# Fetching the first rows with TensorE instead of a DMA, and running the first two blocks on the whole array

## The chip, the cores and the metric

The kernel runs on one core of a Trainium2 chip. The metric is the device time of one execution, in microseconds. Before the change it is 734.75 us, the median of three runs (734.42 to 734.97). The profile comes from a further execution of 734.93 us, in which the core's instructions span 733.2 us; TensorE's granted clock was at full speed throughout.

## The reference

A dynamic convolution over tokens feeds a feed-forward layer with a squared ReLU. `B, S, D = 8, 4096, 192`, with `H = 8` heads of 24 features and `K = 7` taps; the hidden layer has 2048 features.

```python
w = softmax(weight_gen, axis=-1)                    # (B, S, 8, 7)
x_pad = concatenate([zeros(B, 6, D), x], axis=1)
# every token is a weighted sum of itself and the 6 tokens before it;
# the 24 features of one head share the weights
out[b, s, h, :] = sum_k w[b, s, h, k] * x_pad[b, s + k, h, :]
h = maximum(out @ w_in, 0)                          # (32768, 192) @ (192, 2048)
result = h * h @ w_out                              # (32768, 2048) @ (2048, 192)
```

## The kernel before

The tokens go through in blocks: blocks 0 and 1 have 512 tokens each, all others 1024. For each block the kernel does this:

- softmax of the taps on ScalarE and VectorE, into rows `v` (64 numbers for a token: 8 heads with 8 places each);
- "band": the rows of 128 consecutive tokens (`wr`) times a mask give a band matrix `bd` on VectorE, five overlapping tiles for 512 tokens;
- "conv": x times band on TensorE gives `yp`, the convolved tokens with features on the partitions; it is copied out of PSUM into `y`;
- "unit" (`u`): two chunks of 128 hidden features. TensorE computes `h` from `w_in` and `y`, ScalarE takes the ReLU into `t`, VectorE squares it into `g`;
- "M": half of the hidden features of 256 tokens. TensorE multiplies `g` with `w_out` into `o`.

The 192 features do not fill the 128 rows of the array evenly, so the kernel uses three steps of 64 features, and two matmuls stand side by side on the two halves of the rows. For that, `w_in` has to exist a second time with its row halves exchanged (`w_i[:, q, 1]`).

The start, before the first `h`. The softmax has one partition for every 8 tokens (`FIRST = 8`), while the band needs one partition for each token; DMAs do that rearrangement.

```python
# [cut] tiles, helpers
def cross_w_in(q):                      # exchanged halves by DMA
    for r0, r1 in ((0, RT), (RT, 0)):
        nc.sync.dma_start(out=w_i[r0 : r0 + RT, q, 1], in_=w_i[r1 : r1 + RT, q, 0])

def cross_w_in_by_pe(q):                # exchanged halves by a permutation on TensorE
    # [cut] loop over 3 x 512 columns
            nc.tensor.matmul(out=pt[...], lhsT=swap, rhs=w_i[:, q, 0, c : c + TB], ...)
        nc.scalar.copy(out=w_i[:, q, 1, a:b], in_=pt[:, 0 : b - a])

# [cut]
spin(25)                                # TensorE warming matmuls, result unused
half_swap(); band_mask()                # GpSimd
nc.gpsimd.memset(v_big, 0.0)
s0.load(nc.sync)
load_w_in(w_st[0], 0, nc.sync)          # f32, first half of w_in's columns
x_load_f32(0)
load_w_in(w_st[1], 1, nc.sync)
s0.exp(0, s0.rh); s0.total(0, s0.rh); s0.recip(0, s0.rh)
s0.scale(0, s0.rh, nc.vector)           # the rows v are ready here
nc.scalar.copy(out=w_i[:, 0, 0], in_=w_st[0])
wr_load_sbuf(0, [s0], (0, 2, 1, 4, 3), (nc.sync, nc.gpsimd))   # rows of block 0
wr_load_sbuf(1, [s0], range(NT), (nc.gpsimd,))                 # rows of block 1
x_cast(0, nc.scalar.copy)
cross_w_in_by_pe(0)
spin(14)
x_load_f32(1)
nc.scalar.copy(out=w_i[:, 1, 0], in_=w_st[1])
cross_w_in(1)
s1.load(nc.sync)
for i in (0, 2, 1, 3, 4):
    st_band(0, (i,))
st_conv(0)
```

The blocks then follow fixed plans. `B` is a band, `X` a cast of x, `E` and `S` the two halves of a softmax, `C` the convolution of the next block, `L` a load of weights:

```python
plans = {
    0: "B1 X1 u u u E1 S1 u C u u u u",
    1: "L3 u u B2 M E2 B3 u M E2 u u S2 u M u C u S2 M",
    # [cut] the later blocks
}
```

A unit, and the copy of `yp` in block 0:

```python
def st_unit(j, u):
    th = BLOCKS[j][1] * TB // 2         # 256 in blocks 0 and 1, 512 later
    per = TB // th                      # 2 in blocks 0 and 1, 1 later
    # [cut]
    for jj in range(per):
        for slot in range(NK):          # 3 steps of 64 features
            for half, r0 in enumerate((0, RT)):
                k = slot ^ half if slot < 2 else slot
                nc.tensor.matmul(
                    out=h[:, half, jj * th : (jj + 1) * th],
                    lhsT=w_in_chunk(w, u * per + jj, slot, half),
                    rhs=y_t[j][r0 : r0 + RT, k, 0:th], ...,
                    tile_position=(r0, 0),
                )
    # [cut] ReLU and square

# in st_conv, for block 0:
copies = ((0, 2, nc.scalar.copy), (2, NK, nc.vector.tensor_copy))
```

In blocks 0 and 1, `o` uses the full array with 128 rows; from block 2 on it stands on the two row halves.

Of the kernel before, what the change touches and what calls it, by code (L numbers as in the profile page):

```python
# [9 lines left out]
def kernel(  # L10
# [26 lines left out]
    nc = tc.nc  # L37
# [14 lines left out]
    P = 128  # L52
# [2 lines left out]
    NSUB = B * NBB  # L55
    BLOCKS = [(0, 1), (1, 1)] + [(n, 2) for n in range(2, NSUB, 2)]
    NBLK = len(BLOCKS)
    NF = Dff // P

    R = S // P  # L60
# [7 lines left out]
    BASE = -24  # L68
    starts = [BASE + STEP * i for i in range(NT)]
    bounds = [0, 104, 208, 312, 416, TB]  # L70

    AluOp = mybir.AluOpType
    AxisX = mybir.AxisListType.X
# [21 lines left out]
    w_p = const.tile([P, WQ, 2, NQ + NQ // 2], f16, name="w_p")  # L95
    w_o = const.tile([P, NF, Dm], f16, name="w_o")
    mask = const.tile([P, P, 2], f16, name="mask")
    swap = const.tile([P, P], f16, name="swap")
    FIRST = 8
    PARTS = {0: (8, 8, 8, 8), 1: (8, 8, 16), 2: (16, 16)}  # L100
    v_big = const.tile([P, R + 2 * HALO, HP, SL, 2], f16, name="v_big")
    v_first = [
        const.tile([P, FIRST + 2 * HALO, HP, SL, 2], f16, name=f"v_first{i}") for i in (0, 1)
    ]

    def half_swap():

        nc.gpsimd.memset(swap, 0.0)
        for base in (RT, -RT):
            nc.gpsimd.affine_select(  # L110
                out=swap, in_=swap, pattern=[[-1, P]], compare_op=AluOp.not_equal,
                fill=1.0, base=base, channel_multiplier=1,
            )

    def band_mask():

# [22 lines left out]
    def cross_w_in(q):  # L139
        for r0, r1 in ((0, RT), (RT, 0)):  # L140
            nc.sync.dma_start(out=w_i[r0 : r0 + RT, q, 1], in_=w_i[r1 : r1 + RT, q, 0])

    def cross_w_in_by_pe(q):
        n = NQ + NQ // 2
        for a in range(0, n, 2 * TB):
            b = min(a + 2 * TB, n)
            pt = ps_h.tile([P, 2 * TB], f32, name="pt", tag="h")
            for c in range(a, b, TB):
                nc.tensor.matmul(
                    out=pt[:, c - a : c - a + TB], lhsT=swap, rhs=w_i[:, q, 0, c : c + TB],  # L150
                    start=True, stop=True,
                )
            nc.scalar.copy(out=w_i[:, q, 1, a:b], in_=pt[:, 0 : b - a])

    def load_w_spread():

# [197 lines left out]
    def wr_load_sbuf(j, parts, order, engines):  # L354
# [3 lines left out]
        for i in order:  # L358
            t0 = max(j % NBB * TB + tile_start(j, i), 0)
            for s in parts:  # L360
                a, b = max(t0, s.t0), min(t0 + P, s.t0 + P * s.r)
                if a < b:
# [5 lines left out]
                    )  # L368
                    n += 1

    def st_band(j, tiles):


        if j not in bd_t:
            bd_t[j] = p_bd.tile([P, H * NT * STEP], f16, name="bd")
        i = tiles[0]
        lo = STEP * i
        shift = 0 if i == 0 and j % NBB == 0 else lo - tile_start(j, i)
        n = min(STEP, P - shift)
        shape = (P, HP * len(tiles), n // SL, 2 * SL)  # L380
        nc.vector.tensor_tensor(  # L381
            out=bd_t[j][:, H * lo : H * (lo + len(tiles) * n)].rearrange(
                "p (g m c) -> p g m c", g=shape[1], c=2 * SL
            ),
            in0=wr_t[j][:, i : tiles[-1] + 1]
            .rearrange("p t g c -> p (t g) c")
            .unsqueeze(2)
            .broadcast_to(shape),
            in1=mask[:, shift : shift + n]
            .rearrange("p (m c) e -> p m (c e)", c=SL)  # L390
            .unsqueeze(1)
            .broadcast_to(shape),
            op=AluOp.mult,
        )
# [7 lines left out]
    def conv_pieces(j):  # L402


        s0, n = BLOCKS[j]
        th = n * TB // 2
        halves = []
        for half in (0, 1):
            s, a = (s0 + half, 0) if n == 2 else (s0, th * half)
            halves.append([  # L410
                (s, i, half, max(bounds[i], a), min(bounds[i + 1], a + th), a)
                for i in range(NT) if bounds[i] < a + th and bounds[i + 1] > a
            ])
        if n == 2:
            for k in range(NK):
                for later in (True, False):
                    for pair in zip(*halves):
                        for s, i, half, a, b, base in pair:
                            for q in (2 * k, 2 * k + 1):
                                yield later, s, i, q, half, a, b, base  # L420
        else:
            for pair in zip(*halves):
                for later in (True, False):
                    for k in range(NK):
                        for s, i, half, a, b, base in pair:
                            for q in (2 * k, 2 * k + 1):
                                yield later, s, i, q, half, a, b, base

    def st_conv_spread(j):

# [35 lines left out]
    def st_conv(j):  # L466

        if j >= FIRST_SPREAD:
            return st_conv_spread(j)
        n = BLOCKS[j][1]  # L470
        th = n * TB // 2
        per = 1024 // th
        y = p_y.tile([P, NK, TB], f16, name="y")
        y_t[j] = y
        yps = [
            ps_h.tile([P, 2 * TB], f32, name="yp", tag="h") for _ in range(-(-NK // per))
        ]
        for later, s, i, q, half, a, b, base in conv_pieces(j):
            lo = bounds[i]
            hi = lo + (STEP if tile_start(s, i) == starts[i] else bounds[i + 1] - lo)  # L480
            _, ha, hb, pre = quads[q]
            m, h = (32, hb) if later else (pre, ha)
            bd = bd_t[s][:, H * lo : H * hi].rearrange("p (g c e) -> p g e c", g=HP, e=2)
            p0 = RT * half + 32 * (q % 2)
            k = q // 2
            col = th * (k % per) - base
            nc.tensor.matmul(  # L487
                out=yps[k // per][p0 : p0 + m, col + a : col + b],
                lhsT=x_t[s][:, i, 32 * q : 32 * q + m],
                rhs=bd[:, h // 2, h % 2, a - lo : b - lo],  # L490
                start=True,
                stop=True,
                skip_group_check=True,
                tile_position=(0, p0),
            )
        for n, yp in enumerate(yps):
            k0, k1 = n * per, min((n + 1) * per, NK)

            copies = ((k0, k1, nc.scalar.copy),)
            if j == 0:  # L500
                copies = ((0, 2, nc.scalar.copy), (2, NK, nc.vector.tensor_copy))
            for a, b, copy in copies:
                copy(  # L503
                    out=y[:, a:b, 0:th],
                    in_=yp[:, (a - k0) * th : (b - k0) * th].rearrange("p (k c) -> p k c", c=th),
                )

    def st_unit(j, u):

        th = BLOCKS[j][1] * TB // 2  # L510
        per = TB // th
        w = w_p if j >= FIRST_SPREAD else w_i
        h = ps_h.tile([P, 2, TB], f32, name="h", tag="h")
        for jj in range(per):
            for slot in range(NK):
                for half, r0 in enumerate((0, RT)):
                    k = slot ^ half if slot < 2 else slot
                    nc.tensor.matmul(  # L518
                        out=h[:, half, jj * th : (jj + 1) * th],
                        lhsT=w_in_chunk(w, u * per + jj, slot, half),  # L520
                        rhs=y_t[j][r0 : r0 + RT, k, 0:th],
                        start=(jj == 0 and slot == 0), stop=(slot == NK - 1),
                        skip_group_check=True,
                        tile_position=(r0, 0),
                    )
# [22 lines left out]
    def st_mm2(j, qt, fcs, ccs, o):  # L548


        th = BLOCKS[j][1] * TB // 2
        per = TB // th
        half, off = divmod(qt * QT, th)
        for fc in fcs:
            g = g_t[(j, fc // per)][:, half, fc % per * th + off :]
            for cc in ccs:
                n = P // len(o)
                for i, oo in enumerate(o):
# [36 lines left out]
    with nc.allow_low_precision("fp16 matmul pipeline"), tc.manual_schedule():  # L595
# [18 lines left out]
        warm = const.tile([P, TB], f16, name="warm")  # L614
        gate = const.tile([P, 1], f32, name="gate")
        nc.vector.memset(warm, 0.0)
        for v in v_first:
            nc.vector.memset(v, 0.0)

# [2 lines left out]
        def spin(n):  # L622
# [2 lines left out]

        s0, s1, s2 = parts[:3]
        spin(25)
        half_swap()
        band_mask()
        nc.gpsimd.memset(v_big, 0.0)  # L630
        s0.load(nc.sync)
# [1 line left out]
            p_wg.tile([P, (R + HALO) * HK], f32, name="w_st", tag="wg")[:, 0 : NQ + NQ // 2]  # L633
            for q in (0, 1)
        ]
        load_w_in(w_st[0], 0, nc.sync)
        x_load_f32(0)
        load_w_in(w_st[1], 1, nc.sync)
        s0.exp(0, s0.rh)
        s0.total(0, s0.rh)  # L640
        s0.recip(0, s0.rh)
        s0.scale(0, s0.rh, nc.vector)
        nc.scalar.copy(out=w_i[:, 0, 0], in_=w_st[0])
        wr_load_sbuf(0, [s0], (0, 2, 1, 4, 3), (nc.sync, nc.gpsimd))
        wr_load_sbuf(1, [s0], range(NT), (nc.gpsimd,))
        x_cast(0, nc.scalar.copy)
        cross_w_in_by_pe(0)
        spin(14)
        x_load_f32(1)
        nc.scalar.copy(out=w_i[:, 1, 0], in_=w_st[1])  # L650
        cross_w_in(1)
        s1.load(nc.sync)
        for i in (0, 2, 1, 3, 4):
            st_band(0, (i,))
        st_conv(0)

# [1 line left out]
        for q in range(4):  # L658
# [7 lines left out]
        steady = "MuMuuu" * 3 + "MuuuMCu"  # L666
        steady_spread = "MuMuuu" * 2 + "MuCMuuu" + "MuMuuu"
        plans = {
            0: "B1 X1 u u u E1 S1 u C u u u u",
            1: "L3 u u B2 M E2 B3 u M E2 u u S2 u M u C u S2 M",  # L670
            2: "L4 u u u E3 M u u u M B4 u u u u M B5 S3 u u u u M u E3 C u",
            3: "L5 L6 M S3 u u u M u u u u M u M B6 E4 u u u M M B7 u u u E4 M u M C S4 u",
# [109 lines left out]
        for j in range(NBLK):  # L782
            if j + 2 < NBLK:
                load_rows(j + 2)
            u = 0
            for step in plans[j].split():
                kind, n = step[0], int(step[1:] or 0)
# [21 lines left out]
                    st_bands(n)  # L809
                elif kind == "L":  # L810
                    parts[n].load(nc.sync)
                elif kind == "X":
                    x_cast(n, nc.vector.tensor_copy)

# [46 lines left out]
```

The softmax here doesn't subtract the row's maximum and nothing guards it: scores larger than these inputs give would overflow.

## Time and profile before

| What | Value |
|---|---|
| Time, median of three | 734.75 us (734.42 to 734.97) |
| Span in the profile | 733.2 us |
| ScalarE busy in the span | 613.8 us (84%) |
| Warming matmuls, first group | 25, from 1.27 us on |
| Cast of the first half of w_in on ScalarE | 8.06 us, 1.47 us long |
| Start of the first band product | 12.27 us |
| Start of the first `h` matmul | 16.03 us |
| Start of the first square `g` | 19.19 us |
| Start of the first `o` matmul | 26.00 us |
| Start of block 2's first unit | 37.56 us |

How it is read: the page gives busy time by engine for the whole span (PE is TensorE's matmuls, PEld its weight loads, DVE VectorE, ACT ScalarE, POOL GpSimd, SP the engine that issues most DMAs). An engine may be busy without setting the time. So the chain that ended last is read beside it: from the last instruction back to whatever released each step. The share that an engine has in this chain says who sets the end. What happens only in the first 37 us is lost in the averages of a 733 us span; for this the chain, the waits and the busy times are asked of a window, and instructions in order of time. `L381` and the like are lines of the kernel; `x5` is the number of instructions in a group.

### The profile page before, as it was taken

The numbers are of one execution on the slowest core, as the hardware profiler recorded it, in microseconds if no ns is written. First come the engines' busy times: TensorE is split into PE (matmuls) and PEld (weight loads), VectorE is DVE, ScalarE is ACT, GpSimd is POOL, SyncE is SP. The second block draws the span as 40 slices with busy tenths as digits, with TensorE's granted clock in tenths as the row PEclk, the third lists the DMA queues.
The fourth block names the chain that finished last, engine by engine and source line by source line (L and its number), as shares of the span: only waits on it lengthen the run. The fifth ranks groups of instructions, "written<-read, shape, count | busy, mean of one in ns | idle before, by whom it ended". The sixth has DMA issues, their size and how long they took to land.

```text
span 733.2 us, 31124 instructions
## 1 busy us (share of the span) xinstructions
PE 726.3 (99%) x14106; PEld 528.5 (72%) x14106; DVE 627.3 (86%) x856; ACT 613.8 (84%) x724; POOL 100.5 (14%) x148
## 2 busy tenths in 40 slices
PE   8999999999999999999999999999999999999998
PEld 4767777777777777777777777777777777777777
DVE  5999898998898988888988888988889988778753
ACT  5998888988888888888888888888888888888883
POOL 7322222320001100011000010010100110001000
PEclk9999999999999999999999999999999999999999
DMA  7745444794445442455433464334544315444012
GB/s 216 124 88 132 81 63 106 143 164 119 93 73 117 105 86 64 71 131 112 69 70 72 115 125 82 62 68 122 104 87 85 59 49 120 66 87 78 30 45 67
DMA packets 126544, 68.71 MB, mean 94 GB/s; under 512 B 85193, under 2 KB 122636, under 8 KB 125900
## 3 DMA queue, kind: packets, MB, share of 16 engines
q1 hardware_dynamic: 80908, 48.12, 23.0%
q0 software_dynamic: 45360, 18.50, 21.6%
q8 instruction: 110, 1.80, 1.0%
q14 instruction: 22, 0.18, 0.1%
q10 hardware_dynamic: 144, 0.10, 0.0%
HBM read 50.18 MB, written 28.70 MB: 108 GB/s over the span
## 4 chain that ended last, share of the span: by engine, by line
PE 96%; DVE 1%; DMA 1%; ACT 1%; issue 0%; DVEq 0%
PE o L560 47%; PE h L518 45%; PE yp L450 4%; PE yp L487 1%; DVE bd L381 1%; DMA wr<-v_first 1%; ACT t L532 0%; DMA wg<-in_weight_gen_dram 0%; ACT ex L250 0%; DVE v_first L272 0%; ACT y L503 0%; DVE ssum L257 0%; DVE rcp L264 0%; DVE g L536 0%; DVE xt L347 0%
## 5 line engine op out<-in xcount | busy, mean ns | idle before, releaser
L532 ACT ACTIVATE t<-h 128x1024 f16<-128x1024 f32 x512 | 496.5, 1026 | 59.9 <-PE h L518 59.5
L560 PEld LDWEIGHTS <-g 64*128 64x128 f16 (+1 forms) x8032 | 342.5, 94 | 55.9 <-issue 2.5
L560 PE MATMUL o<-w_o,g 64*128 64x192 f16 (+1 forms) x8032 | 379.0, 243 | 0.0
L536 DVE TENSOR_TENSOR g<-t 128x2048 f16<-128x2048 f16 (+1 forms) x309 | 309.3, 1037 | 28.1 <-ACT t L532 27.9
L518 PE MATMUL h<-y,w_p 64*128 64x512 f16 x2400 | 291.7, 376 | 0.0
L518 PEld LDWEIGHTS <-w_p 64*128 64x128 f16 x2400 | 113.8, 94 | 94.9
L381 DVE TENSOR_TENSOR bd<-wr,mask 128x4160 f16<-128x4160 f16 (+3 forms) x89 | 149.4, 1703 | 4.1 <-DMA wr<-v_first 4.1
L576 DVE TENSOR_TENSOR o_sb<-o,o_sb 128x384 f32<-128x384 f32 x123 | 68.4, 556 | 60.8 <-ACT o_sb L574 59.8
L333 POOL DMA_DIRECT2D xt<-in_x_dram x62 | 52.1, 843 | 421.6 <-PE yp L450 362.5
L574 ACT COPY o_sb<-o 128x384 f32<-128x384 f32 x129 | 61.6, 478 | 46.7 <-PE o L560 45.9
L518 PE MATMUL h<-y,w_i 64*128 64x512 f16 (+1 forms) x768 | 82.1, 350 | 1.8 <-ACT t L532 0.8
L518 PEld LDWEIGHTS <-w_i 64*128 64x128 f16 x768 | 36.1, 94 | 28.6 <-issue 4.0
L450 PEld LDWEIGHTS <-xt 128*32 128x32 f16 x2000 | 24.5, 95 | 10.6 <-issue 10.6
L272 DVE TENSOR_TENSOR v_big<-ex,rcp 128x112 f16<-128x112 f32 (+5 forms) x180 | 29.8, 236 | 1.8 <-DMA vd<-v_big 0.8
L460 DVE CAST y<-yp 128x1024 f16<-128x1024 f32 x25 | 30.4, 1218 | 0.0
L450 PE MATMUL yp<-bd,xt 128*32 128x104 f16 (+1 forms) x2000 | 28.3, 210 | 0.0
L250 ACT ACTIVATE ex<-wg 128x560 f32<-128x560 f32 (+4 forms) x38 | 25.9, 682 | 1.7 <-DMA wg<-in_weight_gen_dram 1.7
L257 DVE TENSOR_REDUCE ssum<-ex 128x80 f32<-128x560 f32 (+4 forms) x38 | 25.3, 666 | 2.2 <-ACT ex L250 2.2
L460 ACT CAST y<-yp 128x1024 f16<-128x1024 f32 x25 | 25.2, 1006 | 0.0
L264 DVE RECIPROCAL rcp<-ssum 128x80 f32<-128x80 f32 (+4 forms) x38 | 22.8, 600 | 1.3
L323 POOL DMA_DIRECT2D xt<-in_x_dram x7 | 3.9, 553 | 124.7 <-PE yp L450 109.7
L363 POOL DMA_DIRECT2D wr<-v_first x31 | 16.9, 563 | 16.0 <-DVE v_first L272 15.8
(34 smaller groups left out, 97.3 us busy)
## 6 DMA issues: line engine op xcount, KB each, us to landing
out_dram<-o_sb SPq DMA_DIRECT2D x63, 384.0 KB
xt<-in_x_dram POOLq DMA_DIRECT2D x42, 240.0 KB, 5.0
wg<-in_weight_gen_dram SPq DMA_DIRECT2D x4, 1064.0 KB
xt<-in_x_dram POOLq DMA_DIRECT2D x20, 192.0 KB, 4.7
wr<-vd SPq DMA_DIRECT2D x38, 80.0 KB
vd<-v_big SPq DMA_DIRECT2D x5, 512.0 KB
y<-y SPq DMA_DIRECT2D x100, 24.0 KB
wg<-in_weight_gen_dram SPq DMA_DIRECT2D x5, 392.0 KB
```

What stands on the lines that cost most here:

```text
L250: nc.scalar.activation(out=self.ex[:, lo:hi].rearrange("p r g k e -> p (r g) k e"), in_=self.wg[:, lo:hi].rearrange("p r (g e) k -> p (r g ...
L272: eng.tensor_tensor(out=bass.AP(tensor=v.tensor, offset=v.offset + lo * H * SL + lo % SL * 2 + g * SL * 2, ap=[list(v.ap[0]), [H * SL + 2, ...
L333: eng.dma_start(out=dst[:, first:last], in_=ap)
L381: nc.vector.tensor_tensor(out=bd_t[j][:, H * lo : H * (lo + len(tiles) * n)].rearrange("p (g m c) -> p g m c", g=shape[1], c=2 * SL), in0= ...
L450: nc.tensor.matmul(out=yp[p0 : p0 + 32, k - k0, a:b], lhsT=x_t[s][:, i, c0 : c0 + 32], rhs=bd[:, head // 2, e, 0 : b - a], start=True, sto ...
L460: copy(out=y[:, k0 : k0 + 2], in_=yp)
L518: nc.tensor.matmul(out=h[:, half, jj * th : (jj + 1) * th], lhsT=w_in_chunk(w, u * per + jj, slot, half), rhs=y_t[j][r0 : r0 + RT, k, 0:th ...
L532: nc.scalar.activation(out=t1[:, e], in_=h, func=ActF.Relu)
L536: nc.vector.tensor_tensor(out=g[:, a : e + 1], in0=t1[:, a : e + 1], in1=t1[:, a : e + 1], op=AluOp.mult)
L560: nc.tensor.matmul(out=oo[:, cc * Dm : (cc + 1) * Dm], lhsT=g[r0 : r0 + n, cc * P : (cc + 1) * P], rhs=w_o[r0 : r0 + n, fc, :], start=(fc ...
L574: nc.scalar.copy(out=o_sb, in_=o[0][:, c])
L576: nc.vector.tensor_tensor(out=o_sb, in0=o[1][:, c], in1=o_sb, op=AluOp.add)
```

## The change

It has two parts, both in the first two blocks.

First, the rows of block 0 no longer travel by DMA. A 0/1 matrix `sel` picks from the softmax tile, for each of the five band tiles, the row of each token: 8 accumulating matmuls for a tile (one for each token place in a partition), 64 columns each, into a PSUM tile of its own. ScalarE copies each to `wr`. This is meant to take the DMA's latency out of the start. The rows of block 1 still go by DMA, from two queues now.

Second, blocks 0 and 1 arrange `y` differently. 128 of the features stand on all partitions, so a matmul for them uses the whole array and all 512 tokens; the other 64 features stand twice, once on each row half, and two half-row matmuls run side by side. A unit has 4 matmuls of 512 tokens in place of 12 of 256. No exchanged copy of `w_in` is needed in these blocks, so the permutation on TensorE is dropped and the exchange of both halves by DMA moves to the start of block 1, for use in block 2.

Moves that go with it: x is loaded ahead of `w_in`; x is cast before `w_in`; the second half of `w_in` is cast on VectorE in block 0 (new step `W`); the second group of 14 warming matmuls is gone; the softmax weights of the second part are loaded earlier.

```diff
-    def cross_w_in_by_pe(q): ...                      # [cut]
+    def select_rows(j, s, tiles):
+        wr_t[j] = p_wr.tile([P, NT, HP, SL * 2], f16, name="wr")
+        for n, i in enumerate(tiles):
+            if 0 < n < 4:
+                pr = ps_h.tile([P, H * SL], f32, name="pr", tag="h")
+            else:
+                pr = ps_o.tile([P, H * SL], f32, name="pr", tag=("o1", "o0")[n // 4])
+            a = max(j % NBB * TB + tile_start(j, i), 0) - s.t0
+            for r in range(s.r):
+                c = a + FIRST - 1 - r
+                nc.tensor.matmul(
+                    out=pr, lhsT=sel[:, c : c + P],
+                    rhs=s.v[:, HALO + r].rearrange("p g c e -> p (g c e)"),
+                    start=(r == 0), stop=(r == s.r - 1),
+                )
+            nc.scalar.copy(out=wr_t[j][:, i].rearrange("p g c -> p (g c)"), in_=pr)

+    def st_conv_first(j):                             # [cut] places of the 192 features
+        yp = ps_h.tile([P, 2, TB], f32, name="yp", tag="h")
+        ...
+        if j == 0:
+            nc.scalar.copy(out=y[:, 0], in_=yp[:, 0])
+            nc.vector.tensor_copy(out=y[:, 1], in_=yp[:, 1])
+        else:
+            nc.scalar.copy(out=y[:, 0:2], in_=yp)

+    def first_unit(u, h, y):
+        q, f = divmod(u, NF // WQ // 2)
+        both = [
+            (h[:, n], w_i[:, q, 0, (f + n * NF // WQ // 2) * P :][:, 0:P], y[:, 0], 0)
+            for n in (0, 1)
+        ]
+        upper = [
+            (h[:, n], w_i[r0 : r0 + RT, q, 0, NQ + f * P :][:, 0:P], y[r0 : r0 + RT, 1], r0)
+            for n, r0 in enumerate((0, RT))
+        ]
+        pairs = (upper, both) if u % 2 else (both, upper)
+        ...                                           # [cut] the 4 matmuls

     spin(25)
-    half_swap()
+    row_select()
     band_mask()
     nc.gpsimd.memset(v_big, 0.0)
     s0.load(nc.sync)
+    x_load_f32(0)
     load_w_in(w_st[0], 0, nc.sync)
-    x_load_f32(0)
     load_w_in(w_st[1], 1, nc.sync)
     ...                                               # [cut] softmax, unchanged
+    x_cast(0, nc.scalar.copy)
+    x_load_f32(1)
+    wr_load_sbuf(1, [s0], range(NT), (nc.gpsimd, nc.sync))
+    s1.load(nc.sync)
+    select_rows(0, s0, ROW_ORDER)
     nc.scalar.copy(out=w_i[:, 0, 0], in_=w_st[0])
-    wr_load_sbuf(0, [s0], (0, 2, 1, 4, 3), (nc.sync, nc.gpsimd))
-    wr_load_sbuf(1, [s0], range(NT), (nc.gpsimd,))
-    x_cast(0, nc.scalar.copy)
-    cross_w_in_by_pe(0)
-    spin(14)
-    x_load_f32(1)
-    nc.scalar.copy(out=w_i[:, 1, 0], in_=w_st[1])
-    cross_w_in(1)
-    s1.load(nc.sync)
-    for i in (0, 2, 1, 3, 4):
+    for i in ROW_ORDER:                               # (0, 1, 2, 3, 4)
         st_band(0, (i,))
     st_conv(0)

-            0: "B1 X1 u u u E1 S1 u C u u u u",
+            0: "B1 X1 W u u u E1 S1 u C u u u u",

+            if j == 1:
+                for q in range(WQ):
+                    cross_w_in(q)
+                elif kind == "W":
+                    nc.vector.tensor_copy(out=w_i[:, 1, 0], in_=w_st[1])
```

## The prediction

> **What bounds the kernel now.** I read the page's busy shares first, then the chain that ended last, then the busy time by windows, and only then the start of the span, instruction by instruction, because the change touches nothing after the second block.
>
> ```profile
> PE 726.3 (99%) x14106; PEld 528.5 (72%) x14106; DVE 627.3 (86%) x856; ACT 613.8 (84%) x724; POOL 100.5 (14%) x148
> PE 96%; DVE 1%; DMA 1%; ACT 1%; issue 0%; DVEq 0%
> ```
>
> Over the span TensorE sets the time: 96% of the chain. So a microsecond saved at the start comes out at the end only if TensorE starts its unbroken run earlier, and no other engine holds it up again before that run settles. The windows show where it settles (columns: length, busy PE, PEld, DVE, ACT, POOL with instruction counts, clock, DMA share, GB/s):
>
> ```profile
> 0.00:16.03 16.03, 13.69 (x114) 5.86 (x115) 7.35 (x19) 8.04 (x8) 11.64 (x21) 1.00 0.79 218
> 16.03:26.00 9.97, 8.59 (x192) 6.97 (x192) 9.90 (x20) 8.86 (x11) 5.01 (x8) 1.00 1.18 193
> 26.00:37.56 11.56, 11.56 (x258) 9.65 (x257) 11.47 (x19) 10.44 (x14) 4.54 (x8) 1.00 0.43 73
> ```
>
> The useful TensorE work begins at 16.03 us; block 2 begins at 37.56. What surprised me is VectorE: 9.90 of 9.97 us busy, then 11.47 of 11.56. In blocks 0 and 1 VectorE is as full as TensorE, so whatever the change adds to it there counts. The chain in order of time, for the first 34 us (start, length, what):
>
> ```profile
> 6.70 1.47 DVE v_first L272 x8
> 8.19 3.98 DMA wr<-v_first
> 12.27 2.61 DVE bd L381 x5
> 14.92 0.45 PE yp L487 x16
> 15.40 0.59 ACT y L503
> ...
> 16.36 2.35 DVE bd L381 x2
> 18.70 0.57 DVE xt L347
> ...
> 25.24 0.83 PE h L518 x12
> 26.07 1.43 PE o L560 x16
> ```
>
> The softmax rows are ready at 8.17, the DMA that hands them over takes 3.98 us, the five band products 2.61, the convolution's tail 0.45, the eviction 0.59; then h starts. After that the chain stays on VectorE (bands of the second block, the cast of x), passes through ScalarE and reaches TensorE for good at 25.24. Two waits matter as well (engine and line waited for: us, times, longest):
>
> ```profile
> DVE bd L381 <- DMA wr<-v_first: 4.1, 1, 4.1
> DVE y L503 <- ACT y L503: 1.1, 1, 1.1
> ```
>
> The first is what the change removes. The second: VectorE's share of the eviction of yp does not begin until ScalarE's has ended[...].
>
> [...]16 full-array pairs of 192 columns take 1.43 us in the chain, 89 ns each. No row here has 64 columns on the full array. [...]14 warming matmuls of 512 columns took 3.19 us, 228 ns each[...].
> [...]32 half-row o matmuls among half-row h take 1.32 us in the chain, 16 full-array ones between half-row h 1.43[...]. I take 0.1 us for a switch, an estimate from these differences.
> [...]
>
> **The change part by part.**
>
> 1. Selection in place of the DMA (40 full-array matmuls of 64 columns, 5 ScalarE copies). It may start when the 25 warming matmuls are through, not at 8.17: the last 12 of them stand at 6.79 for 2.85 us, to 9.64, and the swap matmuls start at 9.58. I put the first selection at 9.6. A pair at 70 ns (estimate[...]) gives 40 x 0.07 = 2.8, to 12.4. A copy of 64 columns is an estimate from the 128x512 and 128x1024 copies (588 and 1005 ns, so 0.81 ns a column and 0.17 fixed): 0.22. The last copy ends about 12.75.
>
> 2. Bands and convolution. The bands follow the copies at 0.52 us each (2.60 for 5) against 0.56 for eight pairs, so only the last band is exposed: 12.8 to 13.35, against 14.87. With the convolution tail of 0.45: 13.8, against 15.37. So far 1.5 us earlier.
>
> 3. The cast of w_in stands behind the five copies in ScalarE's order and before the eviction of y. It took 1472 ns: 12.75 to 14.2, beyond 13.8. So this cast, not the convolution, releases y: 14.25 to 14.85 (589 ns, same 128x512 shape). First h at 14.9 instead of 16.03: **1.15 us earlier**. The staged w_in is no obstacle: it landed at 8.06 when first in line, and behind 0.49 MB of x at 256 GB/s (what the window of 4 to 8 us moved) it should land near 10.
>
> 4. VectorE between the first eviction and the first g. It gets the 128x512 half of y in place of 128x256: 0.42 becomes 0.69 (1218 ns for 1024 against 420 for 256 is 1.04 ns a column), +0.27. It gets the cast of the second w_in quarter, 1536 columns at the rate of its x cast (653 ns for 960): +1.04. I read the changed order of instructions as still making the second eviction wait for ScalarE's. So g starts at 19.19 - 1.15 + 0.27 + 1.04 = 19.35, **0.15 us later than before**.
>
> 5. TensorE in the units of blocks 0 and 1. Before: twelve 256-column half-row matmuls, two at a time, 1536 columns deep. After: two full-array matmuls one after the other, 1024 columns, and a half-row pair, 512: again 1536. No columns are saved; 8 issues are[...]. Each unit gains an internal switch; the alternating order makes unit to unit free, and some unit to o junctions. In block 1 I count 13 switches against 10: +0.3 us. In block 0 ScalarE paces (six evictions in 5.66 us, 0.94 each), so the switches hide.
>
> 6. ScalarE: the second block's eviction of y grows from 768 to 1024 columns, 826 to 1012 ns: +0.19. The swap evictions (1.49) and the second w_in cast (1.47) leave it, but both lay in its waiting time.
>
> 7. DMA: all four exchanges of w_in now start in block 1, 0.79 MB at one place instead of half of it at 13.5 us; needed only at block 2.
>
> **Sum.** TensorE's own account at the second convolution (33.87 before): -1.15 + 0.19 + 0.3 = -0.65. VectorE's: the bands of blocks 2 and 3 end at 33.17 before, with no idle time ahead of them, so +0.15 puts them at 33.3 and the convolution at 33.4 at the earliest, about -0.5. The later of the two holds: -0.5. I give 0.2 back for the exchange traffic: **-0.3 us, 734.4**.
>
> **The rivals.**
> (a) The full gain goes through: the selection is quicker (50 ns a pair) and the second eviction doesn't wait. Then h comes near 14.3 and g near 18.5, and -1.2 remains: 733.5. For it: VectorE did have 0.7 us between its bands and the convolution that needs them. Against it: 9.90 of 9.97.
> (b) VectorE eats it all: pairs at 85 ns put h at 15.5 and g at 19.95; the convolution of block 2 starts after 33.9 and nothing is left: 734.8.
> (c) The exchange of w_in, 0.79 MB, falls into the stretch in which the rows of blocks 2 and 3 travel (issued from 24.4 on, landing in 3.0 us at the median). If that landing grows by 2 us, the bands start late while VectorE has nothing else in order: +0.5 to +1, 735.3.
> (d) The array's clock falls. [...]The second run of warming matmuls is gone, and TensorE is half idle from 12.4 to 14.9. The half-idle stretch from 13.3 to 16.0 did not do that before (clock 1.00 throughout). If it did,[...] +1.5, 736.
>
> **Range and chances.** Everything at stake is the start: 16 us of 733, of which at most 4 could go. From (a) to between (c) and (d), with a spread of some 0.5 for my pair time: 733.2 to 735.7. Two per cent is 14.7 us, which no path here reaches: 0.01 faster, 0.98 same, 0.01 slower. Below 734.75 I would put 6 of 10.
>
> **What the changed profile would show.** Step 1: first selection at 9.6 and 40 pairs in 2.8 us; if it starts at 8.2, the warming run was not in the way. Step 3: ScalarE's row of the w_in cast directly before that of y, and y's wait put down to ScalarE; first h near 14.9. Step 4: first g at 19.2 to 19.5, with the cast of w_in before it. Step 5: units of block 1 at 0.75 us against 0.69. Step 7: no wait of the bands for their DMA in block 1. I would be wrong if the first g came before 18.5, or if waits for DMA or a lower clock stood between 14 and 37 us.

## The result, and the profile after

The changed kernel takes 737.09 us (median of six, 736.29 to 737.68) against 734.82 before: ratio 1.0029, 95% interval 1.0016 to 1.0041. It is 2.3 us slower, and outside the predicted range. The profiled execution is one of the quicker ones; its span is 734.9 us, 1.7 longer than before. So the trace can explain 1.7 of the 2.3 us; the rest lies between executions and stays open.

Nearly all of the 1.7 arises before 40 us. Block 2's first unit starts at 39.09 us (37.56 before), 1.53 later; the convolutions from there on keep that distance: 55.03 against 53.51 for the next one, 690.14 against 688.57 for the last.

The page's busy shares and the chain by engine, for the changed kernel:

```profile
PE 725.8 (99%) x14017; PEld 523.6 (71%) x14017; DVE 629.1 (86%) x858; ACT 612.7 (83%) x726; POOL 98.1 (13%) x142
PE 95%; DMA 3%; DVE 1%; issue 0%; POOL 0%; SPq 0%; ACT 0%; DVEq 0%
```

TensorE's busy time is 0.5 us less and its chain share 1% less; DMA has gone from 1% of the chain to 3%. The same three windows as before (length, busy PE, PEld, DVE, ACT, POOL, clock, DMA share, GB/s):

```profile
0.00:16.03 16.03, 13.35 (x159) 6.28 (x159) 8.53 (x20) 7.66 (x12) 8.29 (x14) 1.00 0.87 216
16.03:26.00 9.97, 7.58 (x109) 2.70 (x106) 9.60 (x19) 7.69 (x9) 5.02 (x7) 0.83 1.03 145
26.00:37.56 11.56, 10.84 (x196) 7.02 (x195) 11.49 (x18) 9.48 (x13) 3.89 (x8) 1.00 0.72 140
```

VectorE is as full as before in the last two. TensorE is not: 7.58 busy where it had 8.59, 10.84 where it had 11.56, and its clock fell to a mean of 0.83. The start did become early; from the instructions in order of time (start, length, engine, line, output and inputs, idle time before and its releaser):

```profile
9.09 1.33 PE L371 MATMUL pr<-v_first,sel 128*128 128x64 f16 x40
13.55 3.38 PE L544 MATMUL h<-y,w_i 128*128 128x512 f16 x16 [0.69 <-ACT y L454]
16.34 2.36 DVE L388 TENSOR_TENSOR bd<-wr,mask 128x3328 f16<-128x3328 f16 x2 [2.11 <-DMA wr<-v_first]
```

All 40 selections take 1.33 us, and h starts at 13.55, 2.5 us sooner. Then the bands of block 1 wait 2.11 us for their own rows, which still come by DMA, and start at 16.34. Before, they started at 16.36. Everything won has been spent waiting. The chain in order of time shows what follows:

```profile
10.37 5.84 DMA wr<-v_first
...
18.70 0.57 DVE xt L336
19.27 0.88 DVE w_i L861
20.14 1.80 DVE g L577 x3
21.94 0.89 DVE ssum L246
...
23.74 1.47 DVE v_first L261 x8
...
25.49 1.87 POOL wr L352 x4
...
28.74 6.62 DMA xt<-in_x_dram
...
35.40 1.57 PE yp L514 x110
```

Read downwards: block 1's rows, its bands, the cast of x, the added cast of w_in (0.88 of the chain), the first squares at about 20.1 (19.19 before), the second softmax, whose rows GpSimd can issue only when they exist, and behind them on GpSimd's queue block 3's x: issued at 28.74, landed 6.62 us later. For this the third convolution waits. What TensorE waited for (us, times, longest):

```profile
PE yp L444 <- ACT t L573: 2.4, 1, 2.4
PE yp L514 <- DMA xt<-in_x_dram: 0.7, 1, 0.7
```

The first line is block 1's convolution, held from 16.93 to 19.32 by the late bands and the cast of x (the profile names ScalarE's ReLU, but select_both's convolution starts at 17.76, ahead of its fourth ReLU at 18.63, so it doesn't need that one; what remains is the cast, L336, which ended at 19.26). The second is block 3's x. The last number of the two lines below is what the x load (192 KB) took from issue to landing in us, before and after:

```profile
xt<-in_x_dram POOLq DMA_DIRECT2D x1, 192.0 KB, 4.8
```

```profile
xt<-in_x_dram POOLq DMA_DIRECT2D x1, 192.0 KB, 6.6
```

The sum closes with these. Before: issued at 27.89, landed at 32.7, wanted at 33.87, so 1.2 us of slack. After: 0.85 later to be issued (28.74) and 1.8 slower, less that slack: 1.5 us, which is what block 2 lost.

This sum follows the input that came last. It does not say that everything comes back once x is in time. TensorE in order of time at the third convolution, before and after:

```profile
33.87 1.57 PE L487 MATMUL yp<-bd,xt 128*32 128x104 f16 x120
```

```profile
34.45 0.23 PE L514 MATMUL yp<-bd,xt 128*32 128x104 f16 x2
35.40 1.57 PE L514 MATMUL yp<-bd,xt 128*32 128x104 f16 x118 [0.72 <-DMA xt<-in_x_dram]
```

TensorE itself reached the convolution at 34.45, 0.58 later than before: the first o came 0.42 later (26.42 against 26.00), and the units and o up to the convolution took 0.16 longer. So of the 1.53 us, x's wait holds 0.95, and 0.58 would remain without it.

### The profile page after: what moved, and what is told of

It is laid out like the page before. It is cut to its first block, busy times and chain, and to the rows that moved or that the text cites. A ratio compares the mean times of both kernels' runs of the same rounds, so it can differ in the third digit from the quotient of the medians.

```text
span 734.9 us, 30942 instructions
## 1 busy us (share of the span) xinstructions
PE 725.8 (99%) x14017; PEld 523.6 (71%) x14017; DVE 629.1 (86%) x858; ACT 612.7 (83%) x726; POOL 98.1 (13%) x142
## 4 chain that ended last, share of the span: by engine, by line
PE 95%; DMA 3%; DVE 1%; issue 0%; POOL 0%; SPq 0%; ACT 0%; DVEq 0%
PE o L608 46%; PE h L559 44%; PE yp L480 4%; PE yp L514 1%; DMA w_st<-in_moe_w_in_dram 1%; DMA xt<-in_x_dram 1%; DMA wr<-v_first 1%; POOL wr L352 0%; DVE g L577 0%; DVE v_first L261 0%; DVE ssum L246 0%; DVE w_i L861 0%; DVE rcp L253 0%; PE h L544 0%; SPq L352 0%
## 5 line engine op out<-in xcount | busy, mean ns | idle before, releaser
L559 PE MATMUL h<-y,w_i 64*128 64x512 f16 x576 | 69.6, 376 | 0.0
L559 PEld LDWEIGHTS <-w_i 64*128 64x128 f16 x576 | 26.7, 94 | 24.7 <-issue 0.8
L352 POOL DMA_DIRECT2D wr<-v_first x27 | 14.8, 569 | 15.0 <-DVE v_first L261 12.4
```

The source lines that it names most:

```text
L559: nc.tensor.matmul(out=h[:, half], lhsT=w_in_chunk(w, u, slot, half), rhs=y_t[j][r0 : r0 + RT, k], start=(slot == 0), stop=(slot == NK - 1 ...
```

## The experiments

**Theory.** Three separate things: (1) block 1's rows come by DMA at about 16 us and cap whatever block 0 wins; (2) the cast of w_in on VectorE delays all that VectorE feeds, down to the issue of block 3's x; (3) the exchange of w_in, now issued at 28.48 us, slows the landing of that x. **Rivals:** the clock that fell (0.59 from 20 to 24 us) after TensorE had stood idle; SyncE's queue order; a general saturation of the DMA engines (share 1.05 from 8 to 12.5 us).

One table for all runs. The columns in us are from one profiled execution each: first h, start of block 1's bands, first square, main part of the third convolution, first unit of block 2. Medians and ratios (to the kernel before) are from all executions; the later medians of the kernel before lay at 734.8 to 735.0.

| Run | h | bands 1 | g | conv 3 | block 2 | median | ratio, 95% interval |
|---|---|---|---|---|---|---|---|
| before | 16.03 | 16.36 | 19.19 | 33.87 | 37.56 | 734.82 | |
| changed | 13.55 | 16.34 | 20.07 | 35.40 | 39.09 | 737.09 | 1.0029 [1.0016, 1.0041] |
| rows1_pool | 13.42 | 15.80 | 19.72 | 34.74 | 38.41 | 737.00 | 1.0031 [1.0016, 1.0045] |
| cross_early | 13.58 | 17.40 | 21.13 | 35.38 | 39.48 | 737.80 | 1.0038 [1.0024, 1.0051] |
| keep_warm | 12.79 | 16.99 | 21.00 | 36.20 | 39.90 | 738.16 | 1.0036 [1.0020, 1.0053] |
| cast_first | 13.46 | 16.29 | 19.14 | 34.39 | 38.12 | 736.36 | 1.0018 [1.0009, 1.0028] |
| select_both | 13.89 | 14.48 | 18.71 | 33.26 | 36.93 | 734.36 | 0.9989 [0.9977, 1.0000] |
| x3_first | 12.95 | 16.42 | 20.15 | 35.74 | 39.45 | 735.64 | 1.0000 [0.9990, 1.0009] |
| rows0_dma | 16.88 | 17.47 | 21.17 | 36.62 | 40.29 | 738.21 | 1.0041 [1.0027, 1.0054] |
| conv_late | 13.34 | 17.09 | 19.97 | 35.26 | 40.40 | 736.31 | 1.0023 [1.0011, 1.0035] |
| both_x3 | 14.05 | 14.64 | 18.88 | 34.62 | 39.81 | 735.32 | 1.0005 [0.9995, 1.0016] |
| both_x3_spin | 14.22 | 14.81 | 19.04 | 34.46 | 38.43 | 735.29 | 1.0007 [0.9997, 1.0018] |
| cross_pool | 13.86 | 16.39 | 20.12 | 34.59 | 38.31 | 736.26 | 1.0018 [1.0010, 1.0027] |
| x3_warm | 14.05 | 16.40 | 20.21 | 34.91 | 38.62 | 735.90 | 1.0013 [1.0003, 1.0023] |
| both_cross | 13.51 | 14.10 | 18.33 | 32.59 | 36.27 | 733.50 | 0.9975 [0.9965, 0.9985] |
| both_cross_w2 | 13.12 | 13.71 | 16.62 | 32.91 | 36.58 | 733.97 | 0.9986 [0.9979, 0.9992] |

Of the runs, the seven from rows1_pool to rows0_dma and cross_pool differ from the changed kernel by one edit each, the others by two or more. Executions of one kernel scatter by 1 to 4 us, so single traces are read for their mechanism and medians for the amount. Judged by the intervals, the gains of x3_first and select_both over the changed kernel are clear of the scatter. The gains of cast_first and cross_pool (0.7 and 0.8 us) and the loss of rows0_dma (1.1) are not: there the traces carry the argument. The traces of x3_first, conv_late and both_x3 come from executions that took 1.6 to 2.1 us more than the median of their kernel.

### rows1_pool: block 1's rows on GpSimd's queue alone

```diff
-        wr_load_sbuf(1, [s0], range(NT), (nc.gpsimd, nc.sync))
+        wr_load_sbuf(1, [s0], range(NT), (nc.gpsimd,))
```

> The changed kernel with one edit: the rows of block 1 go on GpSimd's DMA queue alone, as before the change. Queue theory: the two pieces on SyncE's queue arrive late because they stand behind w_in and x there; then block 1's bands start by 14.9 us (16.34 in the changed kernel), the second convolution by 18, TensorE's clock stays at 1.00 from 16 to 26 us, the first o by 25.3 (26.42), time 735.5 to 736.2. Rival, saturation: all DMA engines are full at 8 to 16 us whatever the queue; then the bands start at 16 or later and the time stays at 737.1.

The bands started at 15.80, 0.5 sooner: between the two expectations, and nearer to the second. In this trace block 2 starts 0.68 sooner as well, but the median did not move. So SyncE's queue order explains at most a part of the wait. The landing of the row pieces on GpSimd's queue (size, us from issue to landing), in the kernel before, the changed one and this one:

```profile
wr<-v_first POOLq DMA_DIRECT2D x7, 16.0 KB, 3.2
```

```profile
wr<-v_first POOLq DMA_DIRECT2D x3, 16.0 KB, 6.3
```

```profile
wr<-v_first POOLq DMA_DIRECT2D x5, 16.0 KB, 5.4
```

The same small transfers take 3.2 us before and 5 to 6 after. The change loads block 0's x ahead of w_in, so w_in lands later; and block 1's x and the second softmax's weights are issued earlier (block 1's x from 8.07 us, before from 10.45). All of it now travels while block 1's rows do: from 8 to 12.5 us the DMA share is 1.05, before the change 0.83. Saturation is the better explanation of this wait; no run takes the other loads away to test it alone.

### cross_early: the exchange as soon as each half is cast

```diff
         st_conv(0)
+        cross_w_in(0)
...
                     nc.vector.tensor_copy(out=w_i[:, 1, 0], in_=w_st[1])
+                    cross_w_in(1)
...
-                for q in range(WQ):       # at the start of block 1
-                    cross_w_in(q)
```

> The changed kernel with one edit: the exchange of w_in by DMA is issued as soon as each half is cast (about 12.4 and 20.1 us) and not at the start of block 1 (28.5 us). Collision theory: the exchange slows the load of block 3's x, for which the third convolution waits; then that convolution runs without a DMA wait from about 34.5 us (35.40 in the changed kernel) and the time falls by about 0.9, to 736.2. Rival: the x load is late only because it is issued late on GpSimd; then the convolution still waits until about 35.4 and the time stays at 737.1, or grows if the early exchange delays block 1's rows further.

Each theory had a part right. The third convolution ran in one piece without a DMA wait, though not before 35.38, and block 3's x landed faster than in the kernel before:

```profile
xt<-in_x_dram POOLq DMA_DIRECT2D x1, 192.0 KB, 4.3
```

But the early exchange hit block 1's rows: bands at 17.40 and not 16.34, so the convolution was no sooner, and the time no better. This fits a collision with x; it also shows that this place for the exchange is wrong.

### keep_warm: TensorE's clock alone

```diff
-            0: "B1 X1 W u u u E1 S1 u C u u u u",
+            0: "B1 X1 W u u u E1 S1 u K C u u u u",   # K: 11 warming matmuls
```

> The changed kernel with 11 warming matmuls of 512 columns (about 2.4 us, result unused) put on TensorE between the fourth unit and the second convolution, where it stands idle. Clock theory: the lower clock at 20 to 24 us is a cause of the loss; then with the clock at 1.00 the first o starts at about 25.7 us (26.42) and the time falls by 0.5 to 0.9. Rival: VectorE's order sets the later steps (squares, second softmax, rows, x load, third convolution at 35.4); then the clock is 1.00, the third convolution still starts near 35.4 and the time is unchanged within 0.3 of 737.1.

The window of 20 to 24 us in the changed kernel and here (clock in the last column but two):

```profile
20.00:24.00 4.00, 4.00 (x53) 1.32 (x46) 3.93 (x8) 2.43 (x3) 0.55 (x1) 0.59 1.34 229
```

```profile
20.00:24.00 4.00, 3.97 (x96) 1.76 (x97) 3.96 (x6) 2.85 (x4) 0.32 (x1) 1.00 1.36 232
```

The clock is repaired, and the first o starts at 25.77 instead of 26.42, though the bands came 0.65 later here. TensorE then ran into block 3's x and waited longer for it:

```profile
PE yp L514 <- DMA xt<-in_x_dram: 1.9, 1, 1.9
```

738.16, no gain, and 1.1 above the changed kernel where the rival had allowed 0.3: block 1's rows landed later in this trace, and x was issued later (29.66). With x as the last input, the clock is not what the time hangs on in the changed kernel.

### cast_first: the cast of w_in into VectorE's wait

```diff
-            0: "B1 X1 W u u u E1 S1 u C u u u u",
+            0: "W B1 X1 u u u E1 S1 u C u u u u",
```

> The changed kernel with one edit: on VectorE the cast of the second half of w_in stands ahead of block 1's bands and no longer behind them. VectorE theory: the cast then lies in the 2.1 us in which VectorE waits for block 1's rows, so the first square moves from 20.07 to about 19.1 us, the second softmax's rows, block 3's x load and the third convolution each come 0.9 earlier (35.40 to 34.5), time 736.2. Rival: the x load's landing, not its issue, is what is late (the exchange beside it moves with it), or the clock sets the pace; then the time stays within 0.3 of 737.1.

As the VectorE theory said: first square at 19.14, third convolution at 34.39 without a wait, block 2 at 38.12, median 736.36. The x load landed in 6.6 us here too; it was only issued 0.93 earlier (27.81). So its issue follows VectorE.

### select_both: block 1's rows by TensorE too

```diff
-        wr_load_sbuf(1, [s0], range(NT), (nc.gpsimd, nc.sync))
         select_rows(0, s0, ROW_ORDER)
+        pr1 = select_all(1, s0)          # 5 x 8 matmuls into one PSUM tile
         nc.scalar.copy(out=w_i[:, 0, 0], in_=w_st[0])
+        nc.scalar.copy(out=wr_t[1]..., in_=pr1...)      # 128 x 320
```

(`sel` is 512 columns wider.)

> The changed kernel, but block 1's rows come by TensorE too: 40 more 64-column matmuls into one PSUM tile behind those of block 0, one ScalarE copy of 320 columns, and no DMA for these rows. Theory: their DMA is what turns the early start into a wait. Then block 1's bands start by 14.6 us (16.34 in the changed kernel), the second convolution by 17.6 (19.32), TensorE's clock stays at 1.00, the first square is at about 18.3 (20.07), block 2 starts by 37.2 (39.09), time about 735. Rival: x of block 1 or the second part of w_in lands too late as well, or the x load of block 3 holds the third convolution whatever comes before; then block 2 still starts after 38.2 and the time stays above 736.

The largest single effect. In order of time:

```profile
14.48 2.35 DVE L403 TENSOR_TENSOR bd<-wr,mask 128x3328 f16<-128x3328 f16 x2
33.26 1.56 PE L529 MATMUL yp<-bd,xt 128*32 128x104 f16 x118 [0.87 <-DMA xt<-in_x_dram]
```

The bands follow VectorE's eviction without a wait, the clock stays at 1.00, block 2 starts 2.2 us sooner than in the changed kernel, and the median falls by 2.7 to 734.36. The second line shows what is left: 0.87 us for block 3's x.

### x3_first: block 3's x ahead of the second softmax's rows

```diff
-            0: "B1 X1 W u u u E1 S1 u C u u u u",
+            0: "B1 X1 W u u u E1 u C S1 u u u u",
```

> The changed kernel with the second softmax's VectorE half (step S1) after block 1's convolution instead of before it, so that on GpSimd's queue block 3's x load stands ahead of the second softmax's rows, which wait for VectorE. Queue theory: the x load then is issued at about 21 us (28.74 in the changed kernel), the third convolution runs without a DMA wait from 34.4 (most of it from 35.40 before), and the time falls by 0.9, to 736.2. Rival: the rows come one square later (0.6 us) and the bands of blocks 2 and 3 then hold the convolution instead; no gain, 737.1.

The x load was issued at 22.42, ahead of the exchange (29.16), and landed in 4.8 us:

```profile
xt<-in_x_dram POOLq DMA_DIRECT2D x1, 192.0 KB, 4.8
```

The convolution had no DMA wait; the median fell by 1.45 to 735.64. The amount is above the expected 0.9. The profiled execution (737.24) is the slowest of its twelve, with the clock at 0.50 from 20 to 24 us and 0.81 to 28, so its later columns are no measure of the median.

The other executions of this kernel say more about the clock. The four with a mean clock of 1.000 took 733.19 to 734.65 us, the seven with 0.998 took 735.24 to 736.69: 1.45 us between their medians (734.38 and 735.83). The six of the changed kernel show no such order (737.58 at 1.000, 736.29 to 737.68 at 0.995 to 0.998). cross_pool, where x doesn't hold the convolution either, has 734.70 to 736.28 at 1.000 and 737.28 to 738.86 at 0.995. So once x is no longer the last input, a lower clock goes with a longer time. That it causes it is not shown: rows that land late could stand behind both.

### rows0_dma: the second part of the change alone

```diff
+        wr_load_sbuf(0, [s0], (0, 2, 1, 4, 3), (nc.sync, nc.gpsimd))
         x_load_f32(1)
...
-        select_rows(0, s0, ROW_ORDER)
+        spin(14)
```

> The second part of the change alone: block 0's rows come by DMA as before, on both queues and ahead of block 1's, with the 14 warming matmuls back, and units and convolution on the whole array. If the selection brings nothing in the end because block 1's rows are late anyway, the first h is near 16 us (13.55 in the changed kernel) and the time is no more than 0.5 above the changed kernel's 737.1. Rival: the early start is passed on in part; then the time is 738 to 739.5, as the cast of w_in and the larger eviction on VectorE come on top of the old start.

The rival's range held: h starts at 16.88, 3.3 later than in the changed kernel, and the median is 738.21, 1.1 later. So about a third of the selection's early start reached the end. The clock also fell in this run (0.59 from 16 to 20 us), so the 1.1 may not be the selection's alone. Seen from the kernel before, the larger effect is here: the second part with its moves, without the selection, costs 3.2 to 3.4 us (738.21 against 734.8 to 735.0), and the selection gives about 1.1 back.

### conv_late: work for TensorE while the rows travel

```diff
-            0: "B1 X1 W u u u E1 S1 u C u u u u",
+            0: "W B1 X1 u u u E1 S1 u u u C u u",
```

> The kernel with the cast first (label cast_first, 736.4), and besides block 1's convolution two units later, so that TensorE has units to do while block 1's rows travel. If TensorE's idle 2.4 us and the lower clock after it cost something of their own, the clock is 1.00 at 20 to 24 us, the first o starts at about 25.6 (26.36), block 2 at 37.4 (38.12), and the time is 735.7. Rival: VectorE's order alone sets the third convolution; then block 2 starts at 38.0 to 38.3 and the time stays at 736.4.

The first o started at 24.22, two microseconds earlier than in cast_first, and the third convolution not before 35.26: x again, 2.0 us of waiting. The median is that of cast_first (736.31 and 736.36). The clock fell all the same, only earlier (0.73 from 16 to 20 us) and again from the wait on (0.90 from 32 to 36, 0.67 from 36 to 40). Giving TensorE more to do ahead of a transfer that VectorE releases gained nothing here.

### both_x3 and both_x3_spin: two remedies that collide

Both are select_both with the order of x3_first; the second has `spin(21)` for `spin(25)`.

> The kernel with both blocks' rows by TensorE (label select_both, 734.4), and block 3's x load ahead of the second softmax's rows on GpSimd's queue (as in x3_first). In select_both the third convolution still waited 0.87 us for that load. Theory: with the load early this wait is gone, the third convolution runs through from 32.2 to 32.5 us, block 2 starts by 36.1 (36.93), time 733.5. Rival: the second softmax, one square later, now holds the bands of blocks 2 and 3, and the time stays at 734.4.

> The same as both_x3 with 21 warming matmuls at the start instead of 25, so that the first selection starts at 8.4 us, when its rows are ready, and not behind the warming. If that run is in the way, the first h comes 0.5 earlier and the time is 733.2. Rival: the cast of w_in waits for its load until about 10.5 and sets the first h, or VectorE sets what follows; then the time is that of both_x3.

Neither came below select_both: 735.32 and 735.29. In both_x3:

```profile
30.43 4.59 DVE L403 TENSOR_TENSOR bd<-wr,mask 128x4160 f16<-128x4160 f16 x3 [2.21 <-DMA wr<-v_first]
34.62 2.86 PE L529 MATMUL yp<-bd,xt 128*32 128x104 f16 x118 [1.48 <-DVE bd L403]
```

x no longer waits, but the rows of blocks 2 and 3 now travel beside it and, at the end, beside the exchange (issued at 27.96; the DMA share is 1.32 from 24 to 28 us, 0.87 in select_both): their pieces took 4.3 us to land where they took 2.1 in select_both. The bands wait 2.21, the convolution behind them 1.48. The expected rival (one square later) is a part of it: the rows were issued 0.78 later (24.91 against 24.13). The rest of the wait is their slower landing. The 39.81 in the table also holds a lower clock after that wait (0.82 from 32 to 36 us; the convolution took 2.86 us against 1.86 in both_x3_spin). The trace of both_x3_spin, at a clock of 1.00, has the same two waits (1.89 and 1.48) and rows that landed in 3.8 us. In both_x3_spin the cast of w_in waited 1.7 us for its load, so the shorter warming brought nothing for h (14.22).

### cross_pool: the exchange behind the x load

```diff
                     if j == 0:
                         x_load(3)
+                        # the four exchange DMAs, on nc.gpsimd
...
-                for q in range(WQ):       # on nc.sync, at the start of block 1
-                    cross_w_in(q)
```

> The changed kernel with the exchange of w_in issued on GpSimd's queue right behind block 3's x load instead of on SyncE's beside it. Collision theory: that load lands in 5.0 us or less (6.6 in the changed kernel, 4.8 in the kernel before), the third convolution goes through from 34.5 without a DMA wait, block 2 starts at 38.2 (39.09), time 736.2. Rival: the engines serve the exchange beside the load all the same; landing above 6 us, time 737.1.

The load landed in 4.8 us, as in the kernel before:

```profile
xt<-in_x_dram POOLq DMA_DIRECT2D x1, 192.0 KB, 4.8
```

The third convolution went through without a wait:

```profile
34.59 1.60 PE L514 MATMUL yp<-bd,xt 128*32 128x104 f16 x120
```

Block 2 started at 38.31, the median was 736.26. All as the collision theory had it: beside the exchange 6.6 us, ahead of it in one queue 4.8. Block 2 is still 0.75 later than in the kernel before, close to the 0.58 above that is not x's.

### x3_warm: the clock once x is out of the way

The order of x3_first with the 11 warming matmuls.

> The kernel with block 3's x loaded early (label x3_first, 735.6) and the 11 warming matmuls ahead of block 1's convolution (as in keep_warm). There the clock was repaired but the third convolution still waited for x; here it cannot. If the lower clock costs something once x is out of the way, the clock is 1.00 at 20 to 24 us and the time falls to 735.0. Rival: VectorE's bands of blocks 2 and 3 hold the third convolution at 34.5 either way; then the time stays at 735.6.

735.90, against 735.64 for x3_first: no gain. But the repair was incomplete. The clock was 1.00 from 20 us on, but 0.94 over the first 16 us and 0.82 from 16 to 20. And the warming stood in the way: it kept TensorE until about 21.1, while block 1's x was cast at 19.41, so the convolution started at 21.10 (19.41 in x3_first). So this run does not say what the lower clock costs, and the 1.45 us seen between executions of x3_first stays without a test; a run with no dip and block 1's rows still by DMA is missing.

### both_cross and both_cross_w2: the causes together

both_cross is select_both with the exchange placed as in cross_pool. both_cross_w2 in addition lets GpSimd's DMA cast the second half of w_in on its way (`load_w_in(w_i[:, 1, 0], 1, nc.gpsimd)`) and drops step `W`.

> Two of the found causes removed together: block 1's rows by TensorE (select_both, 734.4) and the exchange of w_in behind block 3's x load on GpSimd's queue (cross_pool). If the causes are separate, the x load lands in 5 us or less (5.8 in select_both), the third convolution goes through from 32.2 us without its 0.87 us wait, block 2 starts at 36.0 (36.93), and the time is 733.5, below the kernel before by 1.5. Rival: as in both_x3, the small row transfers of blocks 2 and 3 then wait instead; block 2 starts no earlier than 36.9 and the time stays at 734.4.

> The same as both_cross, and the second half of w_in is cast to 16 bits on its way in by GpSimd's DMA, so VectorE's cast (1.16 us) is gone. If VectorE still sets the pace in blocks 0 and 1 there, the first square comes near 17.6 us (18.71 in select_both), the bands of blocks 2 and 3 end at 31.4 (32.55), and the time falls by another 0.5 to 1 below both_cross. Rival: TensorE's own run sets it once the waits are gone; then it is the same as both_cross within 0.3, or later if the casting DMA delays the loads of x and w_in at the start.

both_cross takes 733.50 us, 0.25% less than the kernel before (interval 0.15 to 0.35%), and is the best version found:

```profile
13.51 3.38 PE L559 MATMUL h<-y,w_i 128*128 128x512 f16 x16 [0.68 <-ACT y L469]
14.10 2.35 DVE L403 TENSOR_TENSOR bd<-wr,mask 128x3328 f16<-128x3328 f16 x2
32.59 1.56 PE L529 MATMUL yp<-bd,xt 128*32 128x104 f16 x118 [0.59 <-DMA xt<-in_x_dram]
```

Of the 2.5 us won at the first h, 1.29 now arrive at block 2 (36.27). The last 0.59 us of waiting for x is left; it landed in 5.5 us, not under 5. With VectorE's cast gone as well, the first square came at 16.62, and x, issued earlier but landing in 7.6 us, still held the convolution until 32.91: both_cross_w2 is no faster. There the transfers set the pace at the third convolution and VectorE no longer does.

## Why the prediction was wrong

**Step 1** (selection) was mis-sized, on the harmless side. A pair took 33 ns, not 70; 40 took 1.33 us, not 2.8. The 70 was my estimate, and no trace showed it: weight loads last 98 ns each but stand 33 ns apart. That the warming run stands in the way was right (first selection 9.09, rows ready at 8.3).

**Step 2 and 3.** With quick selections the cast of w_in ended at 12.33, ahead of the convolution; y waited for TensorE 0.58 us and not for the cast. h came at 13.55 and not 14.9.

**Step 4 is the one that failed.** Its additions were right: the larger eviction 0.69, the cast 0.96 against 1.04, the second eviction waiting for ScalarE (1.09). What was wrong is the starting point: I moved VectorE's whole chain forward by what h gained, as if block 1's bands depended on block 0 alone. They depend on rows that come by DMA. The kernel before showed no wait there because VectorE reached them only at 16.36; the last of them was issued at 11.8 and, with the landing of 3.2, there by about 15.0 (an estimate). So even unchanged they would have let only some 1.4 of the 2.5 us through, and the loads moved ahead took that too. With rows at 16.34 the gain handed on is 0.02 us, and the cast comes on top: first square 20.07, 0.88 later than before, where I had 0.15. select_both shows it: with these rows by TensorE the bands start at 14.48 and the first square at 18.71.

**Sum.** So both accounts came out late: TensorE reached the third convolution at 34.45 (predicted 33.22), and VectorE's bands for it ended at 33.92 (predicted 33.3). The input that came last, x at 35.36, was in neither.

**Step 5** held: three units of block 1 in a row took 2.27 us up to the next o, 0.76 each (predicted 0.75, before 0.69).

**Step 7 and rival (c)** had the right mechanism and the wrong victim. I gave the exchange 0.2 us and, in the rival, let it slow the rows of blocks 2 and 3 by 2 us. Block 3's x landed 1.8 later; the rows had been issued before the exchange and landed in 1.9 us. cross_pool, with 4.8 us, supports that. The prediction has no account of when x of block 3 was issued and landed, nor of the 1.2 us that it stood from being needed. With VectorE's 0.85 on its issue, that gives the 1.5 us of the trace. The 5.5 us of both_cross, where the load also stands ahead in the same queue, show that the place in the queue isn't the whole story; how the engines share their time between queues is not shown.

**Rival (d)** came true in the trace (clock 0.59 from 20 to 24 us); the +1.5 us I gave it was my estimate, which no trace backed. In the changed kernel no cost of it shows; once x is out of the way, a lower clock goes with 1.45 us (x3_first), and the cause of that stays open. With the waits of 2.11 and 0.72 us for DMA, the prediction's own sign of being wrong, a DMA wait or a lower clock between 14 and 37 us, stood in the trace.

**Rivals (a) and (b)** took TensorE and VectorE as the only candidates. The path ran VectorE, GpSimd's queue, DMA, TensorE, and no account of two engines could find it.

## What to carry to other kernels

A chain shows one releaser a step. Before moving a stage forward, list for every later input how much slack it had: when it was issued, when it landed, when it was used; the smallest slack is all that an earlier start can bring until that input moves too. A transfer moved "to where it isn't needed yet" can slow what is needed there, so try it behind that in the same queue: here x landed in 6.6 us beside the exchange and in 4.8 ahead of it. And a queue that holds an instruction waiting for VectorE can pass VectorE's delay on to the load behind it: here x was issued at 28.74, and at 27.81 with the cast of w_in out of the way (cast_first).

## What the runs showed of the hardware

- Full-array matmuls of 64 columns with a new 128x128 weight each went through at 33 ns a pair (40 in 1.33 us, in all the traces that have them), though a weight load lasts 98 ns (changed kernel).
- 2.4 us without a matmul (16.93 to 19.32, changed kernel) were followed by a lower clock, 0.59 from 20 to 24 us. Depth and moment differed from run to run: at 20 to 24 us 0.50 in x3_first, 0.57 in cross_pool and 0.61 in cast_first; at 16 to 20 us 0.59 in rows0_dma, 0.73 in conv_late and 0.82 in x3_warm. What sets it off is not shown.
- 16 KB row transfers inside SBUF took 1.8 to 6.3 us to land (medians of groups; before and changed kernel), and the 192 KB load of block 3's x from HBM 4.3 to 7.6 us (cross_early and both_cross_w2), with different traffic beside them.
